# A Mamba-2 scan and a SiLU MLP on one core: low parts and differences move from GpSimd to VectorE, and the decay factors are bounded once and read back from DRAM

## The chip, the core and the metric

The kernel runs on one core of a Trainium2 chip. A core has five engines with queues of their own, each in order: TensorE (PE in the rows; PEld is its weight load), VectorE (DVE), ScalarE (ACT), GpSimd (POOL) and SyncE (SP), which here only issues DMAs. They wait for each other by semaphores. The metric is the device time of one execution in microseconds (us).

## The reference

Two blocks follow each other. The first is a Mamba-2 scan over `x` (4 batches, 8 heads, 768 positions, 32 channels), with decays `a` and projections `B`, `C` of 16 states; the second an MLP with SiLU over 3072 tokens of 256 channels and 2048 hidden channels.

```python
log_a = np.log(np.clip(a, 1e-06, 1.0))
for c in range(nc):                      # chunks of 32 positions
    cum = np.cumsum(la, axis=-1)
    L = np.exp(cum[..., :, None] - cum[..., None, :]) * causal
    M = np.einsum('bhin,bhjn->bhij', Cc, Bc) * L
    y[:, :, sl] = M @ xc + (Cc @ state) * np.exp(cum)[..., None]
    state = decay_full * state + sum_j(Bc_j xc_j * decay_from_j)
# (B,H,S,D) -> (B*S, H*D)
h = x @ w_in
g = h * (1.0 / (1.0 + np.exp(-h)))
return g @ w_out
```

Weights arrive as 8-byte floats; everything is returned as 4-byte floats.

## The kernel before

**Units and rounds.** The 3072 tokens are 12 units of 256 positions (three to a batch). Two units make a pair P of 512 tokens, six pairs in all. The MLP of pair 0 is done in plain 4-byte matmuls (`f_s1`, `f_s2`) while the weights come in. Pairs 1 to 5 run in 80 steps, 16 to a pair (f = 0 to 15, one 128-wide slice of the hidden channels each); I call the 16 steps of a pair a round. During the rounds of pairs 1 to 4 the two units of the *next* pair (unit a, unit b) are scanned between the steps; these are the four scan rounds. The round of pair 5 has no scan.

**Split products.** In the rounds every operand is held in three parts: h (the value times a factor a little under one, rounded to TensorE's short float format), l (a low part) and d. A product is three matmuls: h by h and l by l into one PSUM bank, d by d into another place, combined at the end. Weights have WH, WL, WD; the scan's result XH, XL, XD; the hidden layer gh, gl, gd. Before, l comes from GpSimd (`gl` L535, `xl` L472) or VectorE (`wl` L205), and d from h and l (`gd` L539, `xd` L476 on VectorE, `wd` L210 on GpSimd), so that a d waits for its l.

**A step s** issues on TensorE: four matmuls `s1_h` (L521), two of `s1_d` for the next step (L513), four of `s2` three steps back (L553, L554), and two of `s2_d` (L567) for a d-product. ScalarE scales the d-product (L515), takes the SiLU (L529) and makes `gh` (L531). 

**One PSUM tile for three uses.** The four banks `ps_s` hold in turn the scan's products of a unit (`G`, L397, and `D0`, L385), its result `Y` (L437, L446), and the sum of the d-products of the second layer, `b`. So while a unit is scanned the `s2_d` of several steps is held back (PENDING); before the next unit may start, `b` must have been read out: by `f_sum2` (VectorE, L576 and L579), once in the middle of a round and once at its end. The two sums are then combined on GpSimd (`f_sub`, L598).

**The scan of a unit** needs, on VectorE: transposes of B and C (`T`), a bound of the decays laid out by state (`P0`, L291) and their running product `pfx` (`P`, L296), a bound of the decays laid out by position (`0`, L324, L325), two scans `E` (`1`, `2`, L308); on GpSimd `BT` (L341) and `cw` (L369); then on TensorE G and D0, on VectorE the states (`S`, L417) and the product `M` (L403), on TensorE Y. PLAN is a table by f of these letters for units a and b. `load_unit` (`L`) issues a unit's loads on the SP queue; the decays come from the input with each 64-value run repeated over 64 or 16 partitions.

**Start.** Sixteen weight tiles `raw` of 512 KB come through six buffers; ScalarE (`w_size`), VectorE (`w_bits`) and GpSimd (L194) turn them into 4-byte floats. Units 0 to 3 are scanned among the matmuls of pair 0.

Of the kernel before, what the change touches and what calls it, by code (L numbers as in the profile page):

```python
# [29 lines left out]

@with_exitstack
def kernel(
# [67 lines left out]
    def load_pa(u, q):  # L100
        b, t0 = at(u)
        pa[u] = loads.tile([128, UT], FP32, name="pa")
        q.dma_start(out=pa[u], in_=bass.AP(tensor=a.tensor, offset=a.offset + b * H * S + t0,
                                           ap=[[S, H], [0, N], [1, UT]]))

    def load_ab(u, q):
        b, t0 = at(u)
        ab[u] = loads.tile([128, 2, H, Q], FP32, name="ab")
# [736 lines left out]
```

## Time and profile before

| | us |
|---|---|
| median of 2 runs (389.95 to 390.41) | 390.18 |
| the profiled execution | 388.22 |
| its span | 386.5 |
| PE busy in the span | 337.8 |
| DVE, ACT, POOL busy | 254.7, 211.9, 209.0 |
| mean granted TensorE clock | 0.959 |

The page counts an engine as busy while an instruction runs on it; the matmuls overlap, so a busy PE is not one at its peak. The time of an execution is 1.7 us more than the span of its instructions. The granted clock has two levels, 2.4 GHz (1.00) and 1.2 GHz (0.50).

### The profile page before, as it was taken

The numbers are of one execution on the slowest core, as the hardware profiler recorded it, in microseconds if no ns is written. First come the engines' busy times: TensorE is split into PE (matmuls) and PEld (weight loads), VectorE is DVE, ScalarE is ACT, GpSimd is POOL, SyncE is SP. The second block draws the span as 40 slices with busy tenths as digits, with TensorE's granted clock in tenths as the row PEclk, the third lists the DMA queues.
The fourth block names the chain that finished last, engine by engine and source line by source line (L and its number), as shares of the span: only waits on it lengthen the run. The fifth ranks groups of instructions, "written<-read, shape, count | busy, mean of one in ns | idle before, by whom it ended". The sixth has DMA issues, their size and how long they took to land.

```text
span 386.5 us, 7896 instructions
## 1 busy us (share of the span) xinstructions
PE 337.8 (87%) x3146; PEld 263.3 (68%) x3146; DVE 254.7 (66%) x355; ACT 211.9 (55%) x403; POOL 209.0 (54%) x168
## 2 busy tenths in 40 slices
PE   8888699799996799599889879889879899999990
PEld 4566488687775588378668658668658578778880
DVE  6995668968479756958944866944766944325223
ACT  2664478125584367536456646456646456666541
POOL 3444124674649578536835536945536945457440
PEclk9999899989998799969999989999989999999997
DMA  7978963501541400150244150144160120002003
GB/s 141 234 227 180 323 116 95 97 3 41 89 79 37 86 2 0 42 97 2 35 83 75 35 104 2 23 90 82 35 103 2 22 36 0 0 3 40 14 2 55
DMA packets 112619, 26.37 MB, mean 68 GB/s; under 512 B 102214, under 2 KB 108358, under 8 KB 112582
## 3 DMA queue, kind: packets, MB, share of 16 engines
q1 hardware_dynamic: 110502, 25.73, 31.6%
q8 instruction: 25, 0.41, 0.4%
q10 hardware_dynamic: 2080, 0.13, 0.4%
q14 instruction: 12, 0.10, 0.1%
HBM read 22.70 MB, written 3.15 MB: 67 GB/s over the span
## 4 chain that ended last, share of the span: by engine, by line
PE 48%; DVE 30%; issue 9%; ACT 5%; POOL 4%; DMA 2%; DVEq 0%; SPq 0%; POOLq 0%; ACTq 0%
PE hp L521 12%; DVE E L308 8%; PE hp L513 5%; PE b L567 5%; PE oa L554 5%; PE oa L553 5%; DVE gd L539 4%; PE hp L486 4%; PE oa L499 4%; POOL gl L535 3%; PE gy L446 2%; DVE st L417 2%; PE gy L437 2%; DMA raw<-in_moe_w_out_dram 2%; DVE E L403 2%
## 5 line engine op out<-in xcount | busy, mean ns | idle before, releaser
L535 POOL TENSOR_TENSOR gl<-g,gh 128x512 fp32r<-128x512 f32 x80 | 113.0, 1416 | 106.1 <-ACT gh L531 91.6
L539 DVE SCALAR_TENSOR_TENSOR gd<-gl,gh 128x512 fp32r<-128x512 f32 x80 | 75.6, 952 | 96.6 <-POOL gl L535 96.5
L515 ACT ACTIVATE hp<-hp 128x512 f32<-128x512 f32 x80 | 46.5, 581 | 103.6 <-PE hp L513 103.5
L521 PE MATMUL hp<-xh,wh 128*128 128x512 f32 x160 | 67.6, 423 | 1.8 <-ACT hp L515 1.8
L521 PE MATMUL hp<-xl,wl 128*128 128x512 f32 x160 | 65.0, 406 | 0.0
L554 PE MATMUL oa<-gl,wl 128*128 128x512 f32 x160 | 64.1, 400 | 0.0
L553 PE MATMUL oa<-gh,wh 128*128 128x512 f32 x160 | 63.8, 399 | 0.0
L531 ACT ACTIVATE gh<-g 128x512 fp32r<-128x512 f32 x80 | 50.6, 632 | 3.4
L513 PE MATMUL hp<-xd,wd 128*128 128x512 f32 x160 | 52.2, 408 | 0.3 <-ACT g L529 0.3
L529 ACT ACTIVATE g<-hp 128x512 f32<-128x512 f32 x80 | 47.5, 593 | 0.6 <-PE hp L521 0.6
L567 PE MATMUL b<-gd,wd 128*128 128x512 f32 x160 | 45.4, 392 | 0.0
L308 DVE TENSOR_TENSOR_SCAN E<-ab,diag 128x512 f32<-128x512 f32 x24 | 41.0, 1742 | 0.7 <-PE ab L315 0.5
L521 PEld LDWEIGHTS hp<-xh,wh 128*128 128x128 f32 x160 | 31.1, 195 | 12.2 <-ACT hp L515 4.2
L194 POOL TENSOR_TENSOR w<-wu,wv 128x512 uint32<-128x512 uint32 (+1 forms) x20 | 22.5, 1131 | 31.1 <-DVE wv L189 31.1
L513 PEld LDWEIGHTS hp<-xd,wd 128*128 128x128 f32 x160 | 31.0, 195 | 8.3 <-ACT g L529 0.7
L553 PEld LDWEIGHTS oa<-gh,wh 128*128 128x128 f32 x160 | 31.0, 194 | 7.6 <-ACT o L583 0.4
L554 PEld LDWEIGHTS oa<-gl,wl 128*128 128x128 f32 x160 | 30.8, 193 | 7.6
L521 PEld LDWEIGHTS hp<-xl,wl 128*128 128x128 f32 x160 | 31.2, 195 | 6.0
L567 PEld LDWEIGHTS b<-gd,wd 128*128 128x128 f32 x160 | 30.0, 188 | 7.0 <-DVE gd L539 0.3
L486 PE MATMUL hp<-xf,w 128*128 128x256 f32 x128 | 31.5, 401 | 3.6 <-DVE cw L369 1.8
L210 POOL TENSOR_TENSOR wd<-wh,wl 128x512 fp32r<-128x512 f32 x16 | 23.8, 1496 | 13.3 <-DVE wl L205 13.3
L486 PEld LDWEIGHTS hp<-xf,w 128*128 128x128 f32 x128 | 24.7, 199 | 9.1 <-POOL w L194 2.6
(79 smaller groups left out, 420.8 us busy)
## 6 DMA issues: line engine op xcount, KB each, us to landing
ab<-in_a_dram SPq DMA_DIRECT2D x40, 128.0 KB
raw<-in_moe_w_in_dram SPq DMA_DIRECT2D x8, 512.0 KB
raw<-in_moe_w_out_dram SPq DMA_DIRECT2D x8, 512.0 KB
xt<-in_x_dram SPq DMA_DIRECT2D x24, 128.0 KB
out_dram<-ot SPq DMA_DIRECT2D x48, 64.0 KB
bn<-in_B_dram SPq DMA_DIRECT2D x22, 64.0 KB
tbc<-in_C_dram SPq DMA_DIRECT2D x40, 32.0 KB
pa<-in_a_dram SPq DMA_DIRECT2D x10, 128.0 KB
```

Source lines behind the costliest of these rows:

```text
L308: nc.vector.tensor_tensor_scan(out=E[u].rearrange("p k h t -> p (k h t)")[:, Q * g0:Q * (g0 + n)], data0=t.rearrange("p g t -> p (g t)"), ...
L486: nc.tensor.matmul(out=hp[:, i], lhsT=two(w32[j])[:, kc, 128 * i:128 * i + 128], rhs=two(XF[u])[:, kc], start=(kc == 0), stop=(kc == KC - 1))
L513: nc.tensor.matmul(out=HP[s], lhsT=two(WD[f // 2])[:, kc, 128 * (f % 2):128 * (f % 2) + 128], rhs=XD[P][:, kc], start=(kc == 0), stop=Fals ...
L515: nc.scalar.activation(HP[s], HP[s], AF.Copy, scale=-1.0 / UP)
L521: nc.tensor.matmul(out=HP[s], lhsT=two(w[f // 2])[:, kc, 128 * (f % 2):128 * (f % 2) + 128], rhs=x_[P][:, kc], start=False, stop=(kc == KC ...
L529: nc.scalar.activation(G[s], HP.pop(s), AF.Silu, scale=UP)
L531: nc.scalar.activation(GH[s], G[s], AF.Copy, scale=DOWN)
L535: nc.gpsimd.tensor_tensor(out=GL[s], in0=G.pop(s), in1=GH[s].bitcast(FP32), op=ALU.subtract)
L539: nc.vector.scalar_tensor_tensor(out=GD[s], in0=GL[s].bitcast(FP32), scalar=-4096.0, in1=GH[s].bitcast(FP32), op0=ALU.mult, op1=ALU.add)
L553: nc.tensor.matmul(out=OA[P][m], lhsT=two(WH[n])[:, r, ms], rhs=gh, start=(f == 0), stop=False)
L554: nc.tensor.matmul(out=OA[P][m], lhsT=two(WL[n])[:, r, ms], rhs=gl, start=False, stop=(f == NF - 1))
L567: nc.tensor.matmul(out=B2[P][:, m], lhsT=two(WD[n])[:, r, 128 * m:128 * m + 128], rhs=gd, start=(fresh and s == tiles[0]), stop=True, skip ...
```

## The change

Low parts gl are computed on VectorE, except in six of the 16 steps of a scan round (ASIDE), where they stay on GpSimd; xl, wd, BT and cw are on VectorE always. d is computed from h and the value itself instead of from h and l. The decays are bounded once for all units (`f_A2`), written to two DRAM tensors (`a_in`, and `a_zero` with the first value of each run set to 0), and each unit reads them from there: `pz` directly, `ab` in rows of 512 values. `f_sum2` in mid-round is done by ScalarE with a factor; at the end of a round VectorE combines `oa`, the earlier sum and `b` straight out of PSUM, and `f_sub` is gone. PLAN is shifted: D of unit a in step 3 instead of 2, E's second scan and BT in step 3 (FIRST) ahead of that step's gl, transposes of unit a in the step 15 before. At the start `load_unit(2)` stands behind `f_A2`.

```diff
     def load_pa(u, q):
-        pa[u] = loads.tile([128, UT], FP32, name="pa")
-        q.dma_start(out=pa[u], in_=bass.AP(... ap=[[S, H], [0, N], [1, UT]]))
+        for c in range(4):
+            q.dma_start(out=pz[:, c, 1:], in_=a_in[4 * u + c].rearrange("h (o t) -> h o t", o=1).to_broadcast([H, N, Q]))
     def load_ab(u, q):
...
-            q.dma_start(out=ab[u][64 * c:64 * c + 64, k],
-                        in_=bass.AP(... ap=[[0, 64], [S, H], [1, Q]]))
+            q.dma_start(out=ab[u][64 * c:64 * c + 64, k], in_=a_zero[4 * u + t:4 * u + t + 1].to_broadcast([64, H, Q]))
-    def w_d(n, engine=nc.gpsimd):
-        engine.tensor_tensor(out=WD[n], in0=WH[n].bitcast(FP32), in1=WL[n].bitcast(FP32), op=ALU.subtract)
+    def w_d(n):
+        nc.vector.scalar_tensor_tensor(out=WD[n], in0=WH[n].bitcast(FP32), scalar=UP, in1=w32.pop(n),
+                                       op0=ALU.mult, op1=ALU.subtract)
+    acl, acz = (block(n).rearrange("p (h t) -> p h t", t=Q) for n in ("acl", "acz"))
+    for b in range(batch):
+        nc.sync.dma_start(out=acl[NC0 * b:NC0 * b + NC0], in_=bass.AP(... ap=[[Q, NC0], [S, H], [1, Q]]))
+    def f_A2():
+        r = slice(0, NC0 * batch)
+        nc.vector.tensor_scalar(out=acl[r], in0=acl[r], scalar1=1.0, scalar2=1e-6, op0=ALU.min, op1=ALU.max)
+        nc.vector.tensor_copy(out=acz[r], in_=acl[r])
+        nc.vector.memset(acz[r, :, 0:1], 0.0)
+        nc.sync.dma_start(out=a_in, in_=acl[r])
+        nc.sync.dma_start(out=a_zero, in_=acz[r])
...
-    def s1_gl(s):
-        nc.gpsimd.tensor_tensor(out=GL[s], in0=G.pop(s), in1=GH[s].bitcast(FP32), op=ALU.subtract)
+    def s1_gl(s, engine):
+        engine.tensor_tensor(out=GL[s], in0=G[s], in1=GH[s].bitcast(FP32), op=ALU.subtract)
     def s1_gd(s):
-        nc.vector.scalar_tensor_tensor(out=GD[s], in0=GL[s].bitcast(FP32), scalar=-4096.0, in1=GH[s].bitcast(FP32),
-                                       op0=ALU.mult, op1=ALU.add)
+        nc.vector.scalar_tensor_tensor(out=GD[s], in0=GH[s].bitcast(FP32), scalar=1.0 + 1.0 / HALF, in1=G.pop(s),
+                                       op0=ALU.mult, op1=ALU.subtract)
     def f_sum2(P):
+            nc.scalar.activation(SUM2[P][m], b2[:, m], AF.Copy, scale=HALF)
     def f_out(P):
+            if P in SUM2:
+                nc.vector.scalar_tensor_tensor(out=o, in0=OA[P][m], scalar=UP, in1=SUM2[P][m],
+                                               op0=ALU.mult, op1=ALU.subtract)
...
+            nc.vector.scalar_tensor_tensor(out=o, in0=b2[:, m], scalar=-HALF, in1=o, op0=ALU.mult, op1=ALU.add)
-    load_unit(2)
     f_s1(0, 0)
...
     f_s1(0, 2)
+    f_A2()
+    load_unit(2)
-    PLAN = {0: ("aTP0",), 1: ("a12CB",), 2: ("aD",), 3: ("aSsM", "bL"), 4: ("aY",), 5: ("ah", "bTP0"), 6: ("al", "b12CB"),
-            7: ("ad",), 8: ("bD",), 9: ("bSsM", "aL"), 10: ("bY",), 11: ("bh",), 12: ("bl",), 13: ("bd",)}
+    PLAN = {0: ("aPC",), 1: ("a1", "bL"), 3: ("aD",), 4: ("aSsM",), 5: ("aY",), 6: ("ah", "bT"), 7: ("bPC",), 8: ("b1", "aL"),
+            9: ("bD",), 10: ("bSsM",), 11: ("bY",), 12: ("bh", "ald"), 13: ("bld",), 15: ("aT",)}
+    FIRST = {3: "a2B", 9: "b2B"}
+    ASIDE = (2, 4, 5, 6, 10, 15)
...
+            s1_gl(s - 1, nc.gpsimd if f in ASIDE and scans else nc.vector)
             s1_gd(s - 1)
```

VectorE, from the start of a scan round to the product M of unit a. Before (pfx, the bound, two scans, then the reading of `b`):

```order
L291 TENSOR_SCALAR pz<-pa 128x4x64
L296 SCALAR_TENSOR_TENSOR pfx<-pz,one 128x260
L324 TENSOR_SCALAR ab<-ab 128x1024
L325 MEMSET ab 128x16
L539 SCALAR_TENSOR_TENSOR gd<-gl,gh 128x512
L308 SCALAR_TENSOR_TENSOR E<-ab,diag 128x512 x2
L579 TENSOR_TENSOR sum_1496<-b_1709,sum_1496 128x512
L579 TENSOR_TENSOR sum_1497<-b_1709,sum_1497 128x512
L539 SCALAR_TENSOR_TENSOR gd<-gl,gh 128x512 x2
```

With the change:

```order
L311 SCALAR_TENSOR_TENSOR pfx<-pz,one 128x260
L374 TENSOR_TENSOR cw<-ct,pfx 128x256
L540 TENSOR_TENSOR gl<-g,gh 128x512
L544 SCALAR_TENSOR_TENSOR gd<-gh,g 128x512
L324 SCALAR_TENSOR_TENSOR E<-ab,diag 128x512
L595 SCALAR_TENSOR_TENSOR o<-oa,sum_1522 128x512
L595 SCALAR_TENSOR_TENSOR o<-oa,sum_1523 128x512
L602 SCALAR_TENSOR_TENSOR o<-b_1738,o 128x512 x2
L544 SCALAR_TENSOR_TENSOR gd<-gh,g 128x512
L324 SCALAR_TENSOR_TENSOR E<-ab,diag 128x512
L347 TENSOR_TENSOR BT<-bn,E 128x256
L540 TENSOR_TENSOR gl<-g,gh 128x512
```

The reading of `b` now stands between the two scans instead of behind both, and BT, which D0 waits for, behind the second scan on VectorE itself.

TensorE at G (L397, then L402) and D0 (L385, then L390) of unit a in the second scan round. Before:

```order
L521 MATMUL hp<-xl,wl 128x512
L513 MATMUL hp<-xd,wd 128x512 x2
L397 MATMUL gy<-ce,bh 64x128 x16
L385 MATMUL gy<-xt,BT 32x64 x16
L521 MATMUL hp<-xh,wh 128x512
```

With the change (the `oa` rows stand there twice):

```order
L526 MATMUL hp<-xl,wl 128x512
L518 MATMUL hp<-xd,wd 128x512 x2
L558 MATMUL oa<-gh,wh 128x512
L559 MATMUL oa<-gl,wl 128x512
...
L402 MATMUL gy<-ce,bh 64x128 x16
L390 MATMUL gy<-xt,BT 32x64 x16
```

G and D0 moved one step back: the four matmuls of an `s2` (oa) now stand between `s1_d` and G.

The SP queue at the start, from the mark that waits for weight tile 3. Before:

```order
L232 DMA mark<-raw 1x1
L172 DMA raw<-in_moe_w_in_dram 128x2x512 x3
L103 DMA pa<-in_a_dram 128x1x256
L123 DMA tbc_375<-in_C_dram 128x8x16 x2
L123 DMA bn<-in_B_dram 128x8x16 x2
L111 DMA ab<-in_a_dram 64x8x64 x4
L139 DMA xt<-in_x_dram 128x8x32 x2
L172 DMA raw<-in_moe_w_out_dram 128x2x512 x7
```

With the change:

```order
L170 DMA raw<-in_moe_w_in_dram 128x2x512
L243 DMA acl<-in_a_dram 12x8x64 x4
L170 DMA raw<-in_moe_w_in_dram 128x2x512 x2
L170 DMA raw<-in_moe_w_out_dram 128x2x512
L252 DMA a_in<-acl 48x512
L253 DMA a_zero<-acz 48x512
L105 DMA pz<-a_in 128x1x64 x4
L121 DMA tbc_483<-in_C_dram 128x8x16 x2
L121 DMA bn<-in_B_dram 128x8x16 x2
L111 DMA ab<-a_zero 64x512 x4
L137 DMA xt<-in_x_dram 128x8x32 x2
L170 DMA raw<-in_moe_w_out_dram 128x2x512 x6
```

Weight tile 8 (the first of w_out) goes ahead of unit 2's loads, and these wait for the two writes to DRAM.

## Rows read from the trace of the kernel before

**Rows 1.** The page: busy time of each engine, share of the span, instructions.

```profile
PE 337.8 (87%) x3146; PEld 263.3 (68%) x3146; DVE 254.7 (66%) x355; ACT 211.9 (55%) x403; POOL 209.0 (54%) x168
```

**Rows 2.** View of waits: engine, line waited for; total us, times, longest.

```profile
PE gy L397 <- DVE sum L579: 10.6, 3, 3.6
...
PE gy L397 <- DVE sum L576: 5.8, 4, 3.1
...
PE gy L437 <- DVE E L403: 5.5, 5, 2.6
...
PE gy L385 <- POOL BT L341: 2.7, 3, 0.9
```

**Rows 3.** Timeline of PE: start us, duration us, instruction, [idle before it].

```profile
134.64 0.69 PE L437 MATMUL gy<-cw,sm 32*64 32x64 f32 x32 [2.33 <-ACT wh L201]
...
224.30 0.70 PE L397 MATMUL gy<-ce,bh 32*64 32x128 f32 x32 [3.51 <-DVE sum L579]
...
225.28 0.75 PE L521 MATMUL hp<-xh,wh 128*128 128x512 f32 x1
...
228.80 0.40 PE L553 MATMUL oa<-gh,wh 128*128 128x512 f32 x1
...
282.63 0.70 PE L397 MATMUL gy<-ce,bh 32*64 32x128 f32 x32 [3.51 <-DVE sum L579]
```

**Rows 4.** Two stretches: PE, PEld, DVE, ACT, POOL busy (x), PEclk, DMA share, GB/s.

```profile
138.00:140.00 2.00, 2.00 (x10) 1.64 (x9) 1.43 (x1) 1.97 (x5) 2.00 (x3) 1.00 0.00 0
226.00:228.00 2.00, 2.00 (x7) 1.52 (x6) 1.93 (x6) 0.00 (x0) 0.00 (x0) 0.50 0.47 83
```

**Rows 5.** Chain of waits, last round: start us, duration us, piece.

```profile
349.02 0.93 PE hp L521 x4
351.80 0.93 PE hp L521 x4
```

**Rows 6.** Timeline of DVE, third scan round.

```profile
205.97 1.78 DVE L539 SCALAR_TENSOR_TENSOR gd<-gl,gh 128x512 fp32r<-128x512 f32 x1 [3.49 <-POOL gl L535]
...
211.48 0.69 DVE L539 SCALAR_TENSOR_TENSOR gd<-gl,gh 128x512 fp32r<-128x512 f32 x1 [1.43 <-POOL gl L535]
...
219.19 3.87 DVE L308 TENSOR_TENSOR_SCAN E<-ab,diag 128x512 f32<-128x512 f32 x2
```

**Rows 7.** Timeline of POOL beside it.

```profile
205.89 1.31 POOL L472 TENSOR_TENSOR xl<-xf,xh 128x512 fp32r<-128x512 f32 x1
```

**Rows 8.** Groups by line: xcount, busy us, mean ns of one, idle before.

```profile
L535 POOL TENSOR_TENSOR gl<-g,gh 128x512 fp32r<-128x512 f32 x80 | 113.0, 1416 | 106.1 <-ACT gh L531 91.6 <-issue 7.8 <-DVE wl L205 3.6
...
L324 DVE TENSOR_SCALAR ab<-ab 128x1024 f32<-128x1024 f32 x10 | 7.8, 776 | 0.0
```

**Rows 9.** Instructions on tile ab: duration ns min/median/max.

```profile
L308 DVE TENSOR_TENSOR_SCAN E<-ab,diag x24: 1191/1631/2318, 5.4 to 300.8; 128x512 f32<-128x512 f32 x24
```

**Rows 10.** Timeline of PE, start stage.

```profile
40.56 0.44 PE L354 MATMUL tp<-ident,bn 128*128 128x128 f32 x2 [3.74 <-ACT gT L489]
...
46.52 3.69 PE L486 MATMUL hp<-xf,w 128*128 128x256 f32 x16 [1.81 <-DVE cw L369]
...
77.51 0.58 PE L437 MATMUL gy<-cw,sm 32*64 32x64 f32 x24 [2.59 <-DVE E L403]
```

**Rows 11.** Timeline of ACT, start stage.

```profile
38.80 0.66 ACT L178 ACTIVATE wu<-raw 128x512 f32<-128x512 f32 x1 [4.80 <-DMA raw<-in_moe_w_out_dram]
```

**Rows 12.** Timeline of the SP queue, start stage.

```profile
0.80 0.42 SPq L215 DMA_DIRECT2D ach<-in_a_dram  x1
...
22.36 0.65 SPq L103 DMA_DIRECT2D pa<-in_a_dram  x1
...
34.36 7.01 SPq L172 DMA_DIRECT2D raw<-in_moe_w_out_dram  x7
```

**Rows 13.** Timeline of DVE, start stage.

```profile
2.59 0.42 DVE L236 TENSOR_SCALAR ach<-ach 12x512 f32<-12x512 f32 x1 [0.36 <-DMA ach<-in_a_dram]
...
22.80 1.28 DVE L403 TENSOR_TENSOR E<-gy,E 128x512 f32<-128x512 f32 x2
```

More of the change, by code (lines that the diff above doesn't have):

```diff
@@ L28 @@
 UP = 4097.0
+HALF = 4096.0
 @with_exitstack
@@ L93, in acc @@
         return ps_a.tile([128, 512], FP32, name=name, tag="a")
-    pa, ab, bn, tbc, xt = ({} for _ in range(5))
+    ab, bn, tbc, xt = ({} for _ in range(4))
     def at(u):
@@ L572, in f_sum2 @@
         b2 = B2.pop(P)
-        if P not in SUM2:
-            SUM2[P] = [block("sum2") for m in range(2)]
-            for m in range(2):
-                nc.vector.tensor_copy(out=SUM2[P][m], in_=b2[:, m])
-        else:
-            for m in range(2):
-                nc.vector.tensor_tensor(out=SUM2[P][m], in0=b2[:, m], in1=SUM2[P][m], op=ALU.add)
+        SUM2[P] = [block("sum2") for m in range(2)]
+        for m in range(2):
+            nc.scalar.activation(SUM2[P][m], b2[:, m], AF.Copy, scale=HALF)
     def f_out0(m):
@@ L588, in f_out @@
     def f_out(P):
[L590 removed]
+        b2 = B2.pop(P)
         for m in range(2):
             o = block("o")
[L593 to L598 removed]
+            if P in SUM2:
+                nc.vector.scalar_tensor_tensor(out=o, in0=OA[P][m], scalar=UP, in1=SUM2[P][m],
+                                               op0=ALU.mult, op1=ALU.subtract)
+            else:
+                nc.scalar.activation(o, OA[P][m], AF.Copy, scale=UP)
+            OUT.append((P, m, o))
+        for m in range(2):
+            o = OUT[m][2]
+            nc.vector.scalar_tensor_tensor(out=o, in0=b2[:, m], scalar=-HALF, in1=o, op0=ALU.mult, op1=ALU.add)
     def f_store():
[L601 removed]
+        for P, m, o in OUT:
             store(P, m, o)
@@ L754, in step @@
             s1_d(0)
-        def end():
-            s2_d(PENDING)
-            s2(t)
-            PENDING.clear()
-        if ends and scans:
-            end()
         if s < last:
@@ L767, in step @@
         if ends:
-            if not scans:
-                end()
+            s2_d(PENDING)
+            s2(t)
+            PENDING.clear()
             f_out(1 + t // NF)
@@ L780, in step @@
             s2(t)
-        if PENDING and not (scans and (f < 5 or 8 <= f < 11)):
+        if PENDING and not (scans and (f < 6 or 9 <= f < 12)):
             s2_d(PENDING)
             PENDING.clear()
-        if scans and f == 7:
+        if scans and f == 8:
             f_sum2(P)
+        if scans and f in FIRST:
+            stage(2 * P + 2 + "ab".index(FIRST[f][0]), FIRST[f][1:])
         if 1 <= s <= last:
+            s1_gl(s - 1, nc.gpsimd if f in ASIDE and scans else nc.vector)
             s1_gd(s - 1)
         if ends and s >= last:
-            f_sub(nc.vector)
             f_store()
@@ L792, in step @@
             return
-        if t > 2 and t % NF == 2:
-            f_sub()
-        if t > 4 and t % NF == 4:
+        if t > 4 and t % NF == 2:
             f_store()
@@ L799, in step @@
                 u = 2 * P + 2 + "ab".index(what[0])
-                if what[1] == "L":
-                    u += 2 if what[0] == "a" else 0
-                    if u >= 6 and u < NU:
-                        load_unit(u)
-                else:
+                if f == 15 or what == "aL":
+                    u += 2
+                if u < NU:
                     stage(u, what[1:])
```

69 lines of the change are left out of this document (25 added, 44 removed).

## The prediction, made before the changed kernel ran

> **What bounds the kernel now.** I read the page first: PE is busy 337.8 of 386.5 us, DVE and POOL much less [rows 1]. So the question is what keeps PE idle or slow, and the view of waits answers it. PE waits 10.6 and 5.8 us for VectorE to read `b` out of the four-bank tile before G of the next unit may start, 2.7 us for BT on POOL before D0, and 5.5 us for the product M before Y [rows 2]; 2.6 of the last lie before the rounds [rows 10], and one more wait for Y, 2.33 us, ends on ScalarE [rows 3]. Scan rounds thus hold some 10.6 + 5.8 + 2.7 + 5.5 - 2.6 + 2.3 = 24.3 us of waits. Where nothing is scanned, a step takes 351.80 - 349.02 = 2.78 us [rows 5], PE without a gap; there is nothing to win there.
>
> The timeline shows the rest. A scan round (G of unit a to the next one) lasts 282.63 - 224.30 = 58.33 us [rows 3] against 16 x 2.78 = 44.5 us of steps. Behind the longest wait, 3.51 us, the granted clock is 0.50, the 1.2 GHz level [rows 4]; eight matmuls run from 225.28 to 228.80 [rows 3], 3.5 us, where 8/12 of a step would be 1.9. That is 1.7 us a time, four times (one long wait in each scan round): 6.8 us. Waits and slow clock cost about 31 us in the four rounds.
>
> Why is VectorE late there? Its two scans E of a unit take 3.87 us together [rows 6], but a single one has been as short as 1.19 and as long as 2.32 us [rows 9]. In the same way gd takes 0.69 us alone and 1.78 us when it starts with a POOL instruction of 1.31 us [rows 6, 7]: it ends some 0.5 us after that one. Two engines that both do element-wise work in SBUF here take turns. POOL runs one gl a step at 1.42 us on average [rows 8], with xl, cw and the subtraction besides, so VectorE meets it at nearly every step.
>
> **The change, part by part.**
>
> *VectorE's work in a scan round.* I price a two-operand 128x512 instruction alone at 0.65 us (its start-to-start distance, a little under the 0.69 of [rows 6]), a 128x256 one at 0.4 (an estimate, somewhat over half of that), one that reads PSUM at 0.65 too, a scan at 1.19 [rows 9]. Removed per round: two bounds (0.78 each, [rows 8]), two smaller ones, the two `b` readings in mid-round. A round then has 16 gd, 10 gl, two xl and two xd (30 x 0.65 = 19.5), four E (4.8), four instructions for cw and BT (1.6), four out of PSUM at the round's end (2.6), and M, S, pfx and transposes as before (about 10): 38 to 39 us, against 50 or more of PE. The first scan round has nine weight tiles with wl and wd besides (18 x 0.65 = 11.7) and no reading of `oa` for pair 0: about 48. So VectorE has room if it is seldom blocked, and POOL, left with six gl a round (8 us), seldom blocks it.
>
> *The long wait, unit a.* With the change I follow PE from the end of s2 in step 2, when `oa` and `b` are complete. VectorE reads them in four instructions, 2.6 us, and stands waiting for them, with gd, the second E, BT and gl queued behind. PE has s1_h, s1_d (six matmuls, 1.4 us) and s2 of step 3 (0.9) to do, so G waits 2.6 + 0.2 (two signals) - 2.3, about 0.5 us. Then D0 wants BT: behind the readings come gd 0.65, E 1.19 and BT 0.4, so BT is done 5.0 us after s2, while G (0.6) is done at 3.4: 1.6 us of wait. The gl of step 3 is on POOL and becomes ready just about then. If it meets E or BT, the wait grows by what E loses, up to (3.87 - 2 x 1.19)/2 = 0.75 by [rows 6, 9], or by a whole POOL instruction, 1.3 [rows 7]. I take 0.7: G and D0 wait 0.5 + 2.3 = 2.8 us. The ends are 1.6 us (the readings at 0.4 apiece) and 3.4 us.
>
> The Trainium skill ("SBUF — State Buffer", section "Who interferes with whom") says that an instruction of VectorE with two SBUF inputs and a GpSimd instruction that reads SBUF exclude each other for the whole instruction, the earlier one first. By that rule the gl of step 3 blocks E if it is first and BT if it is second, 1.3 us either way, and the wait is 3.4 us, not 2.8: 2.4 us more over four rounds. The slowest E of [rows 9] (1.1 us more than the fastest) fits a whole block better than my 0.7.
>
> *Is the clock then slow?* Three microseconds behind a wait of 2.33 us the clock is 1.00 [rows 3, 4], behind one of 3.51 it is 0.50. Mine lies between, split by G's 32 matmuls into 0.5 and 2.3. I take full clock, close to the edge.
>
> *Unit b.* `b` is read by ScalarE (two at about 0.6 us) while PE does the six matmuls and the s2 of step 9; E1 and E2 stand in steps 8 and 9 with only gl and gd between, so BT is ready first. I take no wait at G, D0 (before: 0.9 each) and Y. What covers them is VectorE keeping up in steps 7 to 11; if it falls back by a step, 2 us return. In the first scan round I add 1.0 for the weight parts.
>
> *Waits that the change could add.* gl is now made a step later, in the queue behind E: s2 uses it two steps on, 5.6 us, and VectorE is never that late by the above. gd no longer waits for gl, which removes most waits of VectorE on POOL; these cost nothing before outside the scans. The SP queue stops at the loads of unit b (`bn` waits for BT of unit a, two steps later); the loads behind it are needed five steps on, and the output stores of step 5 come after. More DMAs per unit (four for pz instead of one) take four times 0.65 us of a queue that is mostly idle in the rounds. ScalarE gives up the two `o` copies and takes the two readings of `b`: no change.
>
> So the rounds: left are 3 x 2.8 + 2.8 + 1.0 = 12 us of the 31. **Gain 19.**
>
> *The start.* Today ScalarE waits 4.80 us for weight tile 8 [rows 11], because its DMA stands behind unit 2's loads (issued from 22.36 us, tile 8 at 34.36 [rows 12]); PE then idles 3.74 us, and 1.81 more for cw of unit 2, and 2.59 before Y of unit 3 [rows 10]. With the change tile 8 is issued ahead of these loads and cw ahead of E. In exchange unit 2's loads wait: for f_A2, which follows M of unit 1 (22.80 + 1.28, [rows 13]) and takes about 1 us, then for the write of `a_in`. The only complete small DMA that I can time, ach, takes from 0.80 to 2.59 us, 1.8 us [rows 12, 13]; behind three weight tiles of 512 KB I allow up to 5 more. So the loads start at 27 to 32 us instead of 22.4 and are issued in about 10 us, the transposes' input first. It is needed at 36.8 (40.56 less the wait): early enough or up to 4 us late. The repeated decays come in 2 KB rows instead of 256 bytes, which shortens unit 2's and unit 3's loads. Bounds: all three waits gone, 8 us and the slow clock behind them, or 2 us lost. VectorE, saturated from there to M of unit 3, gets 18 to 20 more instructions of 0.4 to 0.65 us but is blocked less by POOL. I take **a gain of 5**, nearer the gain since the 4.80 us are a wait on one tile only.
>
> *The end.* After the last matmul stand two instructions of ScalarE, two of VectorE, two transposes and the stores, before and after: 0.
>
> **The sum.** 388.2 (the profiled execution) - 19 - 5 = 364. That execution is 2 us under the median of the two runs, so I say 365 for a median.
>
> **Rivals.**
>
> 1. *The clock falls each round* (0.22). D0's wait is 2.8 to 3.4 rather than 2.3, and the slow stretch stays. For it: by a whole POOL instruction instead of 0.7 the wait is 3.4, next to the 3.51 that did slow it; against it: G in between. 364 + 4 x 1.7 + 4 x 0.6 = 373. The Trainium skill's rule of exclusion above leads here.
> 2. *The DRAM round trip is late* (0.08). Unit 2's transposes wait past 45 us, so that the start loses 2 instead of winning 5: 371; with rival 1 together 380.
> 3. *All scans hide* (0.13). BT is early, the start wins its 8 us: 388 - 31 + 3 - 8 = 352.
> 4. *The wait only moves* (0.07). VectorE, waiting at the readings of step 2 with its whole queue behind it, is late for S and M too, and Y waits what G waited: rounds as before, 385.
> 5. *VectorE becomes the bound; slower* (0.05). At 38.3 us a round it decides from 1.52 times my prices on (58.3 / 38.3). At 1.6, three rounds take 3 us more each, and the first, with 48 us of work, 77 against some 64 (58.3 and the matmuls of pair 0 in its first two steps): 388 + 9 + 13 - 5 = 405. For it: the 1.78 us of gd and the two slow E [rows 6]; against it: gd's 0.69 alone, and that POOL runs six gl a round instead of sixteen and more.
>
> The forecast itself, 357 to 370, has 0.45. The range: from rival 3's 352, a little below it, to rivals 1 and 2 together, 380. Left out are rivals 4 and 5 and what I have not thought of. Two per cent of 390 is 7.8 us, about what a measurement of this kernel can tell from no change: faster means under 382. Forecast and rivals 1 to 3 are faster (0.88), rival 4 the same (0.07), rival 5 slower (0.05).
>
> **What the profile of the changed kernel would show.** PE waits for the reading of `b` at G, about 0.5 us for unit a, not for b; for BT at D0 once a round, about 2.3; not at Y. G of unit a to G of unit a: 53 us. E: 1.2 us each, at most one slow in a round; gd and gl 0.69. PEclk 1.00 in the scan rounds. At the start no wait of ScalarE for a weight tile, and the first step of pair 1 some 5 us earlier. I am wrong if the rounds still last 57 us or more, if VectorE is busy all through them, or if PE's first long wait lies before 45 us and ends on a DMA of unit 2.

## The result, and the profile after

The changed kernel takes 364.37 us (median of 364.23 and 364.51) against 390.18 before; the ratio is 0.934, with a 95 % interval of 0.930 to 0.938. The forecast was 365, the range from a little below 352 to 380. The span falls from 386.5 to 362.7 us and the mean granted clock rises from 0.959 to 0.971. The number was right, in part by luck: its terms were off in both directions, and the experiments show that one part of the change costs about 9 us. Times are medians; one of the four executions of a later run ("decays from the input, tile 8 first") took 356.17 us in a slower state and is left out of its median.

The page after (as [rows 1]): busy time, share of the span, instructions.

```profile
PE 333.4 (92%) x3145; PEld 260.3 (72%) x3146; DVE 259.7 (72%) x430; ACT 211.7 (58%) x403; POOL 64.4 (18%) x56
```

GpSimd has lost 145 us of work and VectorE gained only 5: 75 more instructions, but shorter ones (a gd takes 726 ns on average instead of 952). Its scans show it best (tile E; duration in ns: least, median, most): the median is 1218 instead of 1631 [rows 9]. The second row is BT, now VectorE's: 426 ns as a rule, 1303 at worst.

```profile
L324 DVE TENSOR_TENSOR_SCAN E<-ab,diag x24: 1193/1218/1669, 5.4 to 283.3; 128x512 f32<-128x512 f32 x24
...
L347 DVE TENSOR_TENSOR BT<-bn,E x12: 424/426/1303, 8.4 to 284.5; 128x256 f32<-128x256 f32 x12
```

The view of TensorE's waits (as [rows 2]: total us, times, longest). No wait for the reading of `b` is left; BT ahead of D0 has taken its place, five times, one of them in the start.

```profile
PE gy L390 <- DVE BT L347: 11.2, 5, 2.5
PE hp L526 <- ACT hp L520: 2.6, 2, 1.9
```

The timeline of PE (as [rows 3]): D0 of unit a in scan rounds 2 to 4, and the first matmuls behind one of them.

```profile
158.94 0.46 PE L390 MATMUL gy<-xt,BT 64*32 64x64 f32 x32 [2.24 <-DVE BT L347]
...
208.33 0.69 PE L402 MATMUL gy<-ce,bh 32*64 32x128 f32 x32
211.27 0.43 PE L390 MATMUL gy<-xt,BT 64*32 64x64 f32 x24 [2.25 <-DVE BT L347]
211.63 0.63 PE L526 MATMUL hp<-xh,wh 128*128 128x512 f32 x1
212.06 0.63 PE L526 MATMUL hp<-xl,wl 128*128 128x512 f32 x1
...
265.11 0.46 PE L390 MATMUL gy<-xt,BT 64*32 64x64 f32 x32 [2.25 <-DVE BT L347]
```

From D0 to D0 a round takes 211.27 - 158.94 = 52.3 and 265.11 - 211.27 = 53.8 us, against 58.33 [rows 3]. What stands ahead of BT in VectorE's queue, and the gl on POOL beside it:

```profile
205.66 1.29 DVE L595 SCALAR_TENSOR_TENSOR o<-oa,sum 128x512 f32<-128x512 f32 x2 [2.29 <-PE oa L559]
206.87 1.28 DVE L602 SCALAR_TENSOR_TENSOR o<-b,o 128x512 f32<-128x512 f32 x2
208.06 0.68 DVE L544 SCALAR_TENSOR_TENSOR gd<-gh,g 128x512 fp32r<-128x512 f32 x1
208.66 1.22 DVE L324 TENSOR_TENSOR_SCAN E<-ab,diag 128x512 f32<-128x512 f32 x1
209.91 1.30 DVE L347 TENSOR_TENSOR BT<-bn,E 128x256 f32<-128x256 f32 x1
...
203.32 1.30 POOL L540 TENSOR_TENSOR gl<-g,gh 128x512 fp32r<-128x512 f32 x1 [6.02 <-ACT gh L536]
209.34 1.60 POOL L540 TENSOR_TENSOR gl<-g,gh 128x512 fp32r<-128x512 f32 x1 [4.72 <-ACT gh L536]
```

VectorE stands idle 2.29 us at the readings with E and BT queued behind them. E, begun before gl, takes its 1.22 us, and gl takes 1.60 instead of the 1.30 of the gl before it, beside which VectorE stood idle; BT, begun inside gl, ends at 211.21, just behind gl's end at 210.94: 0.88 us over its 0.42.

The granted clock behind the four waits, rounds 1 to 4 (as [rows 4]; the clock is the third number from the end):

```profile
106.00:108.00 2.00, 2.00 (x7) 1.53 (x6) 2.00 (x5) 0.22 (x1) 0.00 (x0) 0.51 0.82 120
160.00:162.00 2.00, 2.00 (x11) 1.51 (x9) 1.89 (x7) 0.97 (x2) 0.00 (x0) 1.00 0.85 113
211.60:213.60 2.00, 2.00 (x16) 1.59 (x6) 1.93 (x6) 0.00 (x0) 0.00 (x0) 0.56 0.66 64
266.00:268.00 2.00, 2.00 (x7) 1.53 (x7) 1.89 (x7) 0.33 (x1) 0.00 (x0) 0.61 0.79 104
```

It fell in three of four rounds, toward 0.50, the 1.2 GHz level; the two round lengths differ by that, 1.5 us. It fell once more behind TensorE's wait of 1.94 us for ScalarE ahead of the first step of pair 1:

```profile
86.00:88.00 2.00, 2.00 (x6) 1.60 (x5) 0.01 (x1) 0.04 (x1) 0.00 (x0) 0.50 0.15 33
```

The start: the first step of pair 1 begins at 85.24 instead of 88.73 us. The wait for tile 8 [rows 10, 11] is gone, and others stand in its place: TensorE for BT of unit 3, VectorE for tbc of unit 3 (2.02 us at 55.16), since the loads of unit 2 go out at 31.83 instead of 22.36 us. Part of that delay stands ahead of the trip: VectorE waits 2.07 us for `acl` before it may bound the decays. Timelines of PE, of DVE and of the SP queue:

```profile
64.52 0.46 PE L390 MATMUL gy<-xt,BT 64*32 64x64 f32 x32 [1.90 <-DVE BT L347]
...
85.24 0.55 PE L526 MATMUL hp<-xh,wh 128*128 128x512 f32 x1 [1.94 <-ACT hp L520]
...
26.25 0.42 DVE L249 TENSOR_SCALAR acl<-acl 48x512 f32<-48x512 f32 x1 [2.07 <-DMA acl<-in_a_dram]
...
26.70 0.34 SPq L252 DMA_DIRECT2D a_in<-acl  x1
27.29 0.32 SPq L253 DMA_DIRECT2D a_zero<-acz  x1
31.83 2.53 SPq L105 DMA_DIRECT2D pz<-a_in  x4
```

### The profile page after: what moved, and what is told of

It reads as the page before. It is cut to its first block, busy times and chain, and to the rows that moved or that the text cites. A ratio compares the mean times of both kernels' runs of the same rounds, so it can differ in the third digit from the quotient of the medians.

```text
span 362.7 us, 7826 instructions
## 1 busy us (share of the span) xinstructions
PE 333.4 (92%) x3145; PEld 260.3 (72%) x3146; DVE 259.7 (72%) x430; ACT 211.7 (58%) x403; POOL 64.4 (18%) x56
## 4 chain that ended last, share of the span: by engine, by line
PE 67%; DVE 14%; SPq 6%; DMA 6%; issue 3%; ACT 1%; DVEq 0%; ACTq 0%
PE hp L526 21%; PE b L572 10%; PE hp L518 10%; PE oa L559 10%; PE oa L558 10%; DMA raw<-in_moe_w_out_dram 3%; DVE E L324 2%; PE oa L504 2%; SPq L121 2%; DVE wv L187 2%; PE gy L451 2%; DVE BT L347 2%; PE gy L442 1%; DVE wl L203 1%; DMA raw<-in_moe_w_in_dram 1%
## 5 line engine op out<-in xcount | busy, mean ns | idle before, releaser
L540 DVE TENSOR_TENSOR gl<-g,gh 128x512 fp32r<-128x512 f32 x56 | 38.6, 690 | 52.3 <-ACT gh L536 47.2
L540 POOL TENSOR_TENSOR gl<-g,gh 128x512 fp32r<-128x512 f32 x24 | 38.1, 1589 | 188.4 <-ACT gh L536 183.6
L526 PE MATMUL hp<-xh,wh 128*128 128x512 f32 x160 | 66.6, 416 | 2.6 <-ACT hp L520 2.6
L544 DVE SCALAR_TENSOR_TENSOR gd<-gh,g 128x512 fp32r<-128x512 f32 x80 | 57.8, 726 | 9.8 <-ACT gh L536 9.7
L536 ACT ACTIVATE gh<-g 128x512 fp32r<-128x512 f32 x80 | 50.5, 632 | 2.9
L572 PE MATMUL b<-gd,wd 128*128 128x512 f32 x160 | 44.6, 391 | 0.0
L491 PE MATMUL hp<-xf,w 128*128 128x256 f32 x128 | 30.2, 386 | 3.6 <-POOL w L192 2.1
L192 POOL TENSOR_TENSOR w<-wu,wv 128x512 uint32<-128x512 uint32 (+1 forms) x20 | 23.4, 1179 | 50.5 <-DVE wv L187 47.8
L504 PE MATMUL oa<-gT,w 128*128 128x256 f32 x128 | 31.0, 402 | 0.0
L491 PEld LDWEIGHTS hp<-xf,w 128*128 128x128 f32 x128 | 23.4, 190 | 9.2 <-POOL w L192 3.4
```

The lines of the kernel that those rows point to most:

```text
L491: nc.tensor.matmul(out=hp[:, i], lhsT=two(w32[j])[:, kc, 128 * i:128 * i + 128], rhs=two(XF[u])[:, kc], start=(kc == 0), stop=(kc == KC - 1))
L504: nc.tensor.matmul(out=OA[0][m][:, UT * u:UT * u + UT], lhsT=two(w32[8 + j])[:, i, 128 * m:128 * m + 128], rhs=two(GT[u, j])[:, i], start= ...
L526: nc.tensor.matmul(out=HP[s], lhsT=two(w[f // 2])[:, kc, 128 * (f % 2):128 * (f % 2) + 128], rhs=x_[P][:, kc], start=False, stop=(kc == KC ...
L536: nc.scalar.activation(GH[s], G[s], AF.Copy, scale=DOWN)
L540: engine.tensor_tensor(out=GL[s], in0=G[s], in1=GH[s].bitcast(FP32), op=ALU.subtract)
L544: nc.vector.scalar_tensor_tensor(out=GD[s], in0=GH[s].bitcast(FP32), scalar=1.0 + 1.0 / HALF, in1=G.pop(s), op0=ALU.mult, op1=ALU.subtract)
```

## The experiments

Ratios are to the kernel before on the same chip. "First step" is where pair 1 begins, "round" the distance of two D0 (or G) of unit a in the later scan rounds, both from the profile.

| run | us | ratio, 95 % | first step | round |
|---|---|---|---|---|
| before | 390.18 | | 88.7 | 59.4, 58.3 |
| engines alone | 386.50 | 0.992 (0.988 to 0.995) | 86.3 | 60.2, 60.9 |
| order alone | 379.65 | 0.975 (0.972 to 0.979) | 88.8 | 56.0, 55.9 |
| order alone, xd in time | 373.08 | 0.959 (0.953 to 0.965) | 88.3 | 54.1, 53.9 |
| **the change** | 364.37 | 0.934 (0.930 to 0.938) | 85.2 | 52.3, 53.8 |
| all gl on GpSimd | 368.49 | 0.943 (0.938 to 0.949) | 86.7 | 54.4, 54.4 |
| ... and d from l | 369.51 | 0.948 (0.943 to 0.953) | 84.9 | 54.9, 54.7 |
| decays from the input | 365.05 | 0.934 (0.928 to 0.941) | 85.9 | 53.7, 53.9 |
| sums back | 354.62 | 0.912 (0.908 to 0.915) | 85.5 | 50.7, 50.5 |
| gl of step 3 on VectorE | 356.95 | 0.914 (0.909 to 0.919) | 86.3 | 51.5, 51.4 |
| E and BT in step 1 | 352.31 | 0.902 (0.897 to 0.907) | 86.7 | 50.1, 50.0 |
| ... decays from the input, tile 8 first | 351.29 | 0.903 (0.899 to 0.906) | 81.8 | 51.0, 51.0 |
| ... early round trip | **347.67** | 0.893 (0.890 to 0.896) | 81.9 | 50.0, 50.0 |
| ... start shuffled | 348.68 | 0.894 (0.892 to 0.897) | 83.0 | 50.0, 50.0 |

**What is the D0 wait made of? E and BT in step 1.**

```diff
-    PLAN = {0: ("aPC",), 1: ("a1", "bL"), ...
+    PLAN = {0: ("aPC",), 1: ("a12B", "bL"), ...
-    FIRST = {3: "a2B", 9: "b2B"}
+    FIRST = {9: "b2B"}
```

> The second scan E and BT of unit a stand in step 1, ahead of the reading of b, instead of behind it in step 3. Theory: what is left of the wait in a round is BT alone (D0 waits 2.25 us a round, 2.54 in the first, and half clock for about 1.7 us follows); VectorE stands idle 2.29 us before it may read b, room for E (1.2) and BT (0.4). Then D0 waits for nothing, the clock stays at 1.00, and the time falls by about 4 x 4 = 16 us to 349 (346 to 353). Rival: the wait moves to the reading of b, which comes late behind E and BT, so that G waits instead: 358 to 364.

Measured 352.31: the theory, inside its range. The timeline of PE has no wait at G or D0 in rounds 2 to 4:

```profile
204.78 0.69 PE L402 MATMUL gy<-ce,bh 32*64 32x128 f32 x32
205.41 0.43 PE L390 MATMUL gy<-xt,BT 64*32 64x64 f32 x24
205.76 0.50 PE L526 MATMUL hp<-xh,wh 128*128 128x512 f32 x1
```

A round is 50.0 us. So the change's 52.3 is 50.0 plus the wait of 2.25, and its 53.8 has 1.5 of half clock besides. What misses the expected 349 lies ahead of these rounds: the first step 1.4 us later than in the run of the change, in code that is the same, and a wait of 1.37 us for M in round 1.

**GpSimd's part in it. The gl of step 3 on VectorE.**

```diff
-    ASIDE = (2, 4, 5, 6, 10, 15)
+    ASIDE = (2, 5, 6, 10, 15)
```

> Only the gl of step 3 (made in step 4) goes from GpSimd to VectorE in the scan rounds. Theory: BT takes 1.30 us there instead of 0.43 because it stands against that gl on GpSimd; without it D0 waits 2.25 - 0.87 = 1.4 us a round, and the clock, which falls behind 2.25, stays: 4 x (0.87 + 1.7) = 10 us less, 354. If the clock falls all the same: 361. Rival: the 1.30 us have another cause, or VectorE loses the same elsewhere: 364.

Measured 356.95, between the two numbers of the theory; the clock did not fall. The timeline:

```profile
207.36 0.43 PE L390 MATMUL gy<-xt,BT 64*32 64x64 f32 x24 [1.37 <-DVE BT L347]
```

2.25 - 1.37 = 0.88 us, what BT had lost beside that gl.

**Sums out of PSUM on VectorE: undone.**

```diff
+            nc.scalar.activation(o, OA[P][m], AF.Copy, scale=UP)
-                nc.vector.scalar_tensor_tensor(out=o, in0=OA[P][m], scalar=UP, in1=SUM2[P][m], ...)
+                nc.vector.scalar_tensor_tensor(out=SUM2[P][m], in0=b2[:, m], scalar=HALF, in1=SUM2[P][m], ...)
+        if t > 2 and t % NF == 2:
+            f_sub()                       # o - SUM2 on GpSimd
```

> The changed kernel with the sums of unit a's place put back to three engines: ScalarE copies oa out of PSUM, VectorE adds b to the sum held in SBUF (two instructions instead of four in step 2), GpSimd subtracts three steps later, and the stores follow two steps later than that. Theory: the four readings on VectorE stand ahead of E and BT, so two fewer make BT 1.29 us earlier; D0 waits 0.96 instead of 2.25 us four times, and the clock does not fall behind it (three times 1.5 us): 364.4 - 5.2 - 4.5 = 354.7 us (352 to 358). The move of the sums to VectorE alone would then have cost time. Rival: ScalarE's copies come late (behind its two instructions on g), s2 of step 3 waits for oa's buffers and the D0 wait turns into that one: 362 to 366.

Measured 354.62, the theory by its number. Its waits came out otherwise: in place of 0.96 us at D0 in each round there is none in rounds 2 to 4, and the change's 2.54 us in round 1, whose pair has no earlier sum and which the edit leaves as it was. VectorE reads `b` alone, so BT is done before G (timelines of DVE and PE; what is left at PE is 0.28 us for ScalarE):

```profile
202.71 1.22 DVE L324 TENSOR_TENSOR_SCAN E<-ab,diag 128x512 f32<-128x512 f32 x1
203.96 0.42 DVE L347 TENSOR_TENSOR BT<-bn,E 128x256 f32<-128x256 f32 x1
...
202.99 0.73 PE L518 MATMUL hp<-xd,wd 128*128 128x512 f32 x2 [0.28 <-ACT g L534]
...
205.20 0.43 PE L390 MATMUL gy<-xt,BT 64*32 64x64 f32 x24
```

This part of the change, in its place, costs 364.37 - 354.62 = 9.75 us, or, by the two ratios, each against the kernel before on its own chip, (0.934 - 0.912) x 390 = 8.6 us: about 9.

**Place or engine? The order alone, in the kernel before.**

```diff
-    PLAN = {0: ("aTP0",), 1: ("a12CB",), 2: ("aD",), 3: ("aSsM", "bL"), ... 8: ("bD",), ... 12: ("bl",), 13: ("bd",)}
+    PLAN = {0: ("aTP0",), 1: ("a12CB",), 3: ("aD",), 4: ("aSsM", "bL"), ... 9: ("bD",), ... 13: ("bl",), 14: ("bd",)}
```

> The kernel before with one edit: in a scan round every step of the schedule from D of unit a on is put one step later (D of unit a in step 3 instead of 2, D of unit b in step 9 instead of 8, b read in step 8), and the wd parts of the second layer are gathered one step longer. Nothing changes its engine, its operands or its loads; GpSimd keeps gl, xl, BT, cw and the subtraction. Theory (place, not engine): G no longer meets the reading of b at once, since a whole step of 2.78 us lies between, so its wait of 3.51 us falls to about 0.7 and the 1.7 us of half clock behind it go; unit b keeps its waits of 0.9 at G and at D0. 4 x (3.5 + 1.7 - 0.7) = 18: 372 us (367 to 377). Rival (the engines matter): VectorE, blocked by a GpSimd that runs a gl in every step, is late wherever the step is put: 383 to 390.

Measured 379.65, between both. The wait at G of unit a is gone in rounds 2 to 4, but my edit made xd late (timeline of PE):

```profile
220.03 0.69 PE L397 MATMUL gy<-ce,bh 32*64 32x128 f32 x32
...
240.81 0.70 PE L397 MATMUL gy<-ce,bh 32*64 32x128 f32 x32 [1.23 <-DVE sum L576]
...
261.74 0.71 PE L513 MATMUL hp<-xd,wd 128*128 128x512 f32 x2 [1.69 <-DVE xd L476]
```

So it was run again with `12: ("bh", "bl"), 13: ("bd",)`.

> The order alone once more, with the low parts of unit b's x made where they were in time: xl in step 12 behind xh, xd in step 13 (379.65 us with xl in 13 and xd in 14, where TensorE waited 1.69 us a round for xd, and 0.67 and 0.28 behind it). Theory: these 2.6 us go in each of the four rounds and nothing takes their place, so a round is 53.3 instead of 55.9 us, and the order alone, with all work left on GpSimd, makes the rounds as short as the whole change does: 379.65 - 10.5 = 369 us (367 to 373). Rival: xl, now ahead of a gl on GpSimd, delays that gl and with it s2, and the wait only moves: 376 to 381.

Measured 373.08, the upper end of the theory's range. Rounds of 54.1 and 53.9 us stand within 0.1 to 1.8 us of those of the whole change, with every gl, xl, BT, cw and subtraction still on GpSimd, and with E still slow there (median 1640 ns). The clock stays at 1.00 in these two rounds, so the fair match is the change's 52.3: order alone makes a round 4 to 5 us shorter, the rest of the change some 1.7 us more.

**The engines alone, in the kernel before.**

```diff
-    def f_B(u, engine=nc.gpsimd):          # f_xl, w_d, f_C likewise
+    def f_B(u, engine=nc.vector):
-        nc.gpsimd.tensor_tensor(out=GL[s], ...
+        engine = nc.gpsimd if s % NF in (1, 3, 4, 5, 9, 14) and 2 + s // NF < NP else nc.vector
+        engine.tensor_tensor(out=GL[s], ...
```

> The kernel before with the engines alone: BT, cw, xl, wd and ten of sixteen gl of a scan round on VectorE (all gl of the last round), six gl and the subtraction left on GpSimd, every instruction in the place and with the operands that it had, and the decays bounded unit by unit. Theory (place first): in the kernel before, b is complete at 219.2 us while VectorE starts E at that moment and reads b behind it; E then takes 2.4 instead of 3.87 us, but BT, cw and a gl join it on VectorE, so the reading moves by less than 1 us, G still waits some 2.5 to 3 us and the clock still falls; unit b loses its waits of 0.9. 381 us (376 to 386). Rival (engine first): VectorE, no longer blocked, catches up by a whole step and reads b in time: 366 to 373.

Measured 386.50, on the side away from the rival and past the theory's range. The wait, for which I expected 2.5 to 3 us, grows, from 3.51 to 4.20 us: cw and BT now stand in VectorE's queue ahead of the reading, and the two E still take 3.35 us, not 2.4. Unit b's wait at G, which the theory had gone, grows as well, from 0.94 to 2.45 us. Timelines of DVE and PE:

```profile
214.79 3.35 DVE L308 TENSOR_TENSOR_SCAN E<-ab,diag 128x512 f32<-128x512 f32 x2
218.07 0.39 DVE L369 TENSOR_TENSOR cw<-ct,pfx 128x256 f32<-128x256 f32 x1
218.38 0.41 DVE L341 TENSOR_TENSOR BT<-bn,E 128x256 f32<-128x256 f32 x1
218.72 1.28 DVE L580 TENSOR_TENSOR sum<-b,sum 128x512 f32<-128x512 f32 x2
...
220.05 1.16 PE L397 MATMUL gy<-ce,bh 32*64 32x128 f32 x32 [4.20 <-DVE sum L580]
...
244.36 0.70 PE L397 MATMUL gy<-ce,bh 32*64 32x128 f32 x32 [2.45 <-DVE sum L577]
```

What the engines do give by themselves is the start: 86.3 instead of 88.7.

**All gl on GpSimd, then d from l as well, in the changed order.**

```diff
-            s1_gl(s - 1, nc.gpsimd if f in ASIDE and scans else nc.vector)
+            s1_gl(s - 1, nc.gpsimd)
```

> All 80 gl on GpSimd again, everything else as in the changed kernel. Theory: GpSimd then meets VectorE at every step, E and the two-operand instructions take up to 1.1 us more, E and BT late, and the rounds lose a good part of what they won: 370 to 378. Rival: the gain came from the order alone (b read ahead of the second E, D a step later, the sums out of PSUM), and it does not matter where gl is made: 363 to 366.

368.49: between the two, 4.1 us over the change. D0 of unit b waits 0.43 to 0.48 us a round, 1.8 us in all, and the clock falls in all four rounds, 1.5 us more than in the change, behind a wait that is no longer than there (2.23 us). With gd made of gh and gl:

> All gl on GpSimd in the changed order (368.5 us), and besides gd made from gl again (gh/4096 - gl) instead of from gh and the value itself, so that every gd on VectorE waits for a gl on GpSimd. It prices that part of the change by itself. Theory: with GpSimd running a gl a step, gd waits about 1.5 us in most steps, and what stands behind it on VectorE is late by that much: BT of unit b and the readings of step 2; two to three waits of TensorE a round grow by 0.7 to 1.5 us: 374 us (371 to 380). Rival: VectorE has that much slack in each step, as it had before the change, and only the place of E, BT and the readings counts: 367 to 370.

369.51: the rival. In the view of waits VectorE stands 100 us for GpSimd, and that is worth 1 us, less than the intervals of the two runs can tell apart:

```profile
DVE gd L545 <- POOL gl L540: 100.0, 56, 4.9
```

**The round trip through DRAM: undone.**

```diff
-            q.dma_start(out=pz[:, c, 1:], in_=a_in[4 * u + c]...)        # ab from a_zero likewise
+        q.dma_start(out=pa[u], in_=bass.AP(tensor=a.tensor, ...))         # bounded by unit, as before
+    load_unit(2)
     f_s1(0, 0)
...
-    f_A2()
-    load_unit(2)
```

> The decays come from the input again, with a bound for each unit on VectorE, and unit 2's loads are issued behind weight tile 7, as before the change; all else as changed. Theory: the start loses what it won, since weight tile 8 is late again: 3.5 us; the rounds gain or lose little, as the bounds (about 1 us a unit) find room on VectorE, up to 1 us a round where they stand ahead of E: 367 to 372. Rival: the round trip through DRAM costs more than it saves (unit 3's transposes wait 3.4 us for it), and without it the time is 360 to 363.

365.05: between the two, and the same as the change itself; this part moves nothing. TensorE's wait for tile 8 is back (3.48 us at 40.58), and the late loads of unit 3 are gone with the trip: the first step at 85.9 against 85.2. In the rounds, the bounds lie in the 2.29 us for which VectorE waits anyway (1.41 us of them are left).

**The start, with E and BT in step 1.** First the decays from the input, but tile 8 ahead of unit 2's loads (`load_unit(2)` behind `w_bits(2, 2)`):

> Loads of the decays from the input, bounded unit by unit (no round trip through DRAM), the scans and BT of unit a in step 1, and besides the loads of unit 2 one place later in the queue, behind weight tile 8 instead of ahead of it. Theory: at the start the wait for tile 8 (3.48 us on TensorE with the loads ahead of it) goes, unit 2's input is still in time, and nothing else of the start is late: with the rounds at 50.0 us the time is some 3.8 us under that of the scans alone, 348.5 us (346.5 to 350.5). Rival: the loads, which start at about 24.5 instead of 22.4 us, make unit 2's transposes late, or unit 3's loads, and the wait only moves: 351 to 353.5.

351.29: the rival by its number, not by its reason. The first step comes 4.9 us earlier, more than the theory had; but the rounds are 51.0 instead of 50.0 us, because the bounds, 1.05 us of VectorE a unit, no longer lie in a wait: VectorE stands idle nowhere between them and the reading, and G waits for it (PE, G of round 2):

```profile
152.01 0.70 PE L394 MATMUL gy<-ce,bh 32*64 32x128 f32 x32 [0.47 <-DVE o L594]
```

Then the trip kept but early: `acl` loaded on ScalarE's queue at the top, `f_A2` behind `f_Ek(1, 0)`, `load_unit(2)` behind `w_bits(2, 2)`.

> The round trip through DRAM kept, the scans and BT of unit a in step 1, and the trip made early: the small loads of all decays are issued on ScalarE's queue at the very start, the three instructions that bound them follow the first scan of unit 1, and the loads of unit 2 stand behind weight tile 8. Theory: what was late at the start (the pieces of unit 2 at 31.8 us, then tbc and ab of unit 3) was late because a_in was written at 26.7 us; written at about 20 us, the loads start about 7 us earlier and the waits of 1.2 us for bn, of 1.3 and 1.4 for tbc and of 2.1 for BT of unit 3 go or shrink: 348 to 350 us. Rival: the loads are late for their bytes and packets, not for their start (tbc of unit 3 has one buffer), or VectorE, with three instructions more in its busiest stretch, holds up unit 1: 351 to 354.

347.67, the theory, a little under its range. The SP queue:

```profile
22.01 0.41 SPq L252 DMA_DIRECT2D a_in<-acl  x1
22.52 0.37 SPq L253 DMA_DIRECT2D a_zero<-acz  x1
...
27.15 3.25 SPq L105 DMA_DIRECT2D pz<-a_in  x4
```

The waits for bn, for tbc and at D0 of unit 3 are gone. The first step comes as early as in the run just above, a round is shorter by 1.0 us, and this is the fastest version, faster than both kernels. Last, two moves more, of `f_A2` behind `w_bits(1, 2)` and of `4:T` ahead of `l5 d5`:

> The early round trip and the early scans (347.7 us), with two moves at the start: the bounds of the decays stand behind the three instructions of weight tile 1 instead of ahead of them, and the two transposes of unit 4 stand ahead of wl and wd of tile 5 instead of behind them. Theory: of TensorE's wait of 2.1 us for weight tile 1 about 1 us goes; ct of unit 4 is ready 1.3 us earlier, so that ScalarE, which waits for it, comes earlier to the first product of pair 1, and TensorE's wait there of 1.94 us shrinks to about 0.6: 345.5 us (344 to 346.5). Rival: the pieces of unit 2 come later by as much as tile 1 comes earlier, and wl and wd of tile 5 are late in turn: 347 to 349.

348.68: the rival. TensorE's wait ahead of the first product shrank from 1.94 to 0.70 us, but D0 of unit 3 waits 1.81 us again: `a_in`, now issued behind three weight tiles instead of two, went out at 23.95 us and `pz` at 31.31, a trip of 7.4 instead of 5.1 us.

## Why the prediction was right, point by point

- **The rounds, "53 us instead of 58.33".** Right: 52.3 at full clock, and 53.8 where the clock fell. The 58.33 is the shortest of the rounds before; the one ahead of it, from G to G, lasted 59.4, the first 64.9. Of the parts, the readings ahead of BT and a blocked VectorE instruction were priced at 1.6 + 0.7 us at D0; the runs have 1.37 + 0.88 (gl of step 3 moved away). E goes first and keeps its 1.2 us, BT is the one blocked, not E.
- **"G and D0 wait 0.5 + 2.3 = 2.8 us."** 0 + 2.25. The 0.5 at G failed: VectorE begins at 205.66, when the first half of oa is complete, not behind the second, and is done at 208.1, as TensorE ends s2 of step 3.
- **"I take full clock, close to the edge."** This step failed: the clock fell in three of four rounds, 1.5 us each, as rival 1 has it, though behind waits of 2.25 and 2.54 us and not of 3.4, and with a time of 364 and not of its 373.
- **"Gain 19" in the rounds.** 20.3: the span is 23.8 shorter, the first step 3.5 earlier. Left are 9.3 us of waits at D0 (2.54 + 2.24 + 2.25 + 2.25), 0.7 for ScalarE and four falls of the clock (the one behind the first step of pair 1 among them) at 1.5, together 16 instead of 12; so the rounds before held about 36 us to lose, not 31. I had added up the waits for VectorE and GpSimd and one for ScalarE; three more for ScalarE, 2.96 us, stand in the same timeline of PE before:

```profile
159.59 0.50 PE L521 MATMUL hp<-xh,wh 128*128 128x512 f32 x1 [0.89 <-ACT hp L515]
...
253.96 0.58 PE L437 MATMUL gy<-cw,sm 32*64 32x64 f32 x24 [1.15 <-ACT g L529]
...
312.05 0.69 PE L437 MATMUL gy<-cw,sm 32*64 32x64 f32 x32 [0.92 <-ACT hp L515]
```

  And I had priced the slow clock at 1.7 us four times. The mean clock over ten microseconds around the four long waits (the third number from the end) gives 1.7 = 10 x (1 - 0.83) in rounds 3 and 4 alone, and 3.4 in rounds 1 and 2, 0.4 to 0.5 of it while TensorE still waited:

```profile
120.00:130.00 10.00, 6.94 (x70) 5.01 (x70) 8.29 (x8) 3.62 (x7) 8.71 (x7) 0.66 0.38 67
161.00:171.00 10.00, 6.39 (x77) 4.72 (x76) 8.27 (x12) 4.07 (x8) 4.94 (x4) 0.66 0.45 86
222.00:232.00 10.00, 7.70 (x96) 5.87 (x100) 6.68 (x11) 4.92 (x11) 3.17 (x3) 0.83 0.57 101
280.00:290.00 10.00, 7.37 (x84) 5.57 (x84) 6.72 (x11) 4.96 (x11) 3.48 (x4) 0.83 0.59 100
```

  The other way, 0.8 us of the waits for M in my 24.3 lie before the rounds. What was to be lost and what was left were both too small, and that they nearly cancel is luck.
- **Unit b, no waits; first round 1.0 more.** Right for unit b. Round 1 has 2.54 at D0, 0.3 over the others and not 1.0.
- **"Why is VectorE late there?"** The prediction named E's and gd's turns with POOL. The turns are real (E's median 1631 to 1218 ns), but the runs put the gain elsewhere: D of unit a a step later makes rounds of 54 us with every turn left in, while the engines moved with the old order make the wait longer. In the new order the move of gl is worth 4.1 us at most (all gl back: 368.49), 1.5 of them by a fall of the clock behind an equal wait; xl, wd, BT and cw were not moved back there. At the start the engines alone are worth 2.4 us.
- **The trade named in the forecast's own text**, readings queued ahead of E and BT, is what was left in the rounds: about 9 us come back with the sums undone, 12 with E and BT ahead of the readings.
- **The start, "a gain of 5".** 3.5 in the profiled run, 2.1 to 3.9 in five others with the same start; in the profiled run 1.5 of it goes again in half clock behind the first step. Tile 8's wait went as said; the loads of unit 2 started at 31.8, the late end of "27 to 32 us", and made unit 3's late, which I had not followed. Undoing both, the trip and the place of tile 8, leaves the gain as it was (85.9), and tile 8 ahead without the trip gives 81.8: what the place of tile 8 won, the late trip gave back. What is left of the gain fits the engines: alone they give 2.4, with tile 8 as late as ever (TensorE waits 5.3 us ahead of the transposes).
- **The rule of exclusion** (the Trainium skill, "SBUF — State Buffer", section "Who interferes with whom"), by which the wait would be 3.4 us: the trace agrees in who gives way (gl, begun inside E, and BT, begun inside gl) and not in the size. Of the 0.54 us that gl ran beside E it lost 0.30, and of the 1.03 us that BT ran beside gl it lost 0.88, so neither stood still for the whole time. And what BT can lose is only what is left of gl when it begins, not the whole 1.3 that I took.
- **VectorE as the bound** (rival 5): 39.3 us busy in the round of 52.3, as priced (38 to 39).

## What to carry to other kernels

When the tensor engine waits for another engine, look first at what stands ahead in that engine's queue and at the step in which the waiting instruction is placed; here the old kernel won 16.6 us (389.70 to 373.08) when the scan's steps were put one later, and 3.4 us (389.89 to 386.50) when 138 us of work were taken off GpSimd (209.0 to 71.1 us busy). A sum read out of PSUM by the engine that also makes the next matmul's operand, and ahead of it in the queue, puts all of it ahead of that matmul. And undo each part of a change by itself: the sums cost time in their place, and the trip through DRAM was worth nothing until it was made early. Whether the sums gain anything once E and BT stand ahead of them was not run.

## What the runs showed of the hardware that I had not expected

- **Where the clock falls is not a fixed wait.** In five runs (the change, all gl on GpSimd, d from l as well, decays from the input, sums back) D0 of unit a waited 2.23 to 2.54 us 17 times in all; the granted clock fell behind 14 of them and stayed at 1.00 behind three (2.24, 2.54 and 2.54 us), as it did behind the 2.33 us before [rows 3, 4]. It never fell behind the four waits of 1.37 and 1.66 us at the same place (gl of step 3 on VectorE). Ahead of the first step of pair 1 it fell behind four waits of 1.93 to 1.96 us and not behind two of 1.94 and 1.96. What decided between equal waits stays open.
- **A write to DRAM and the read of it behind each other on one queue** took 31.83 - 26.70 = 5.1 us from issue to issue with other loads under way, the same 5.1 us (27.15 - 22.01) when it was made earlier, and 31.31 - 23.95 = 7.4 with one weight tile more issued ahead of it; that the tile is the reason was not tested.
- **One start, six times:** with the same code, the first step came at 84.9, 85.2, 85.5, 86.3, 86.7 and 86.7 us, and with the start of the kernel before, three times, at 88.3, 88.7 and 88.8. A microsecond at the start is not evidence.
